# The first chunk of an LSH-attention and MLP kernel in two parts, and some conversion work on GpSimd

## The chip, the cores and the metric

The kernel runs on one core of a Trainium2 chip. The metric is the device time of one execution in microseconds (us). A core has five engines that run their own instruction streams and wait for one another by semaphores: TensorE (PE; its weight loads are listed apart as PEld), VectorE (DVE), ScalarE (ACT), GpSimd (POOL) and SyncE (SP), which here only starts transfers. Instructions of one engine run in the order in which they stand.

## The reference

```
q_bits = (q @ proj) > 0 ; k_bits = (k @ proj) > 0          # 6 bits each
mask   = bucket(q_bits)[:, None] == bucket(k_bits)[None, :]
scores = where(mask, q @ k.T / sqrt(64), -1e9)
attn   = softmax(scores) @ v
x      = attn of the 8 heads side by side                  # 3072 x 512
h      = x @ w_in ; g = where(h > 0, h, exp(min(h, 0)) - 1)
out    = g @ w_out
```

There are 4 batches, 8 heads, 768 rows, 64 values per head; `w_in` is 512 x 2048, `w_out` 2048 x 512. Inputs are float32, and the weights come as 64-bit floats of which the kernel makes 32-bit ones itself. The weight matrices, the MLP and the softmax are as in the reference; all matrix products run in 16-bit floats, each operand split into a hi part and a lo part (the rest), so that one product is three matmuls.

## The kernel before, in words

**Work items.** A *pair* is two heads of one batch; four pairs make a batch. A *chunk* is half of the rows of a batch (3 of its 6 tiles of 128 rows, `HC = 3`), for all four pairs; there are eight chunks. For each pair and chunk, `pair_part` does six tiles of attention (3 row tiles for each of two heads), two at a time (a *duo*): PE makes the scores (tile `ss` or `os`, lines 776 to 789), DVE copies them out of PSUM with their maximum (`top`, line 796), ACT takes the exponential (819), ACT makes the hi part of the normalised row (tile `hl`, line 844 through helper line 217), DVE the lo part (847 through helper line 220), and a transposing DMA on SP turns it into tile `PT`. When the six tiles have landed, PE multiplies with V (`av`, 867 to 879), and ACT and DVE make the hi and lo parts of `x` (888, 891).

**The experts (the MLP).** `moe_part` needs `x` of all four pairs of its chunk. For each of 16 slices `f` of the 2048 hidden columns PE makes `h` (12 matmuls, line 940), five elementwise steps follow (`e1` ACT 956, `e2` POOL 960, `e3` DVE 963, `e4` ACT, `e5` DVE through the helper lines 217 and 220), and PE adds to the three output tiles `o` (9 matmuls, line 988).

**The weights.** 32 blocks of 128 x 512 are loaded in `w_part` by SP into three or four buffers, decoded (ACT 695, DVE 699 and 703), bounded (PE `acc`, 714), and, when all 16 of one matrix have been bounded and its scale is known (`w0s`, `w1s`), split: hi on ACT, lo on DVE (745 to 752).

**Early work.** The first chunk's Q and K are turned by PE instead of DMA, and their hash bits are made by `bits_early`: PE multiplies with the projection into tile `zh` (line 481), DVE compares with zero (line 485). The projection itself is prepared by `prep_proj` (255 to 280), which starts with its own two small transfers, on ACT's queue.

**What sets the order.** Every step is a `job` with an engine, an estimated time, a key and what it waits for; `run_plan` (122 to 187) plays the jobs through with the constants of lines 31 to 48 (hops between engines, leads of the early loads, keys) and writes each engine's instructions in the order it finds. A change of a constant can so move any instruction.

## Time and profile before

| | us |
|---|---|
| median of 3 runs (lowest, highest) | 902.96 (902.17, 907.09) |
| the profiled execution | 905.69 |
| its span, first to last instruction | 903.9 |

| engine | busy us | share | instructions |
|---|---|---|---|
| PE | 821.7 | 91% | 5161 |
| DVE | 704.3 | 78% | 1482 |
| ACT | 699.1 | 77% | 1360 |
| POOL | 125.8 | 14% | 179 |

The page cuts the span into 40 slices of 22.6 us and prints a digit for each engine and slice: its busy share in tenths. A row of a table by stage gives, for a stretch of the span, the busy time of each engine with its number of instructions in brackets, then the granted TensorE clock (PEclk, 1.00 is full), the busy share of the DMA engines and what they moved. A row of a group of instructions gives line, engine, operation, the tile written and the tiles read, the shapes and the count; then the busy time of the group and the mean of one instruction in ns; then the idle time of the engine just before these instructions and what ended it.

### The profile page before, as it was taken

What the parts mean: (1) busy time and instruction counts of PE and PEld (TensorE: products, weight loads), DVE (VectorE), ACT (ScalarE), POOL (GpSimd) and SP (SyncE); (2) the same over time, 40 slices, a digit from 0 to 9 for tenths busy, and PEclk for the clock granted to TensorE, in tenths of its full rate; (3) what the DMA queues carried; (4) which work ended last, traced back from release to release, by engine and by line L of the source; (5) the groups of instructions that cost most, each with busy time, mean ns of one, the idle gap of its engine ahead of it and who ended that gap; (6) DMA issues with size and microseconds to landing.
All of it is one profiled execution on the core that took longest, in us unless ns stands there. A gap on an engine that the chain in (4) does not pass through costs nothing.

```text
span 903.9 us, 14772 instructions
## 1 busy us (share of the span) xinstructions
PE 821.7 (91%) x5161; PEld 431.0 (48%) x5161; DVE 704.3 (78%) x1482; ACT 699.1 (77%) x1360; POOL 125.8 (14%) x179
## 2 busy tenths in 40 slices
PE   2767565999999999999999999999999999999996
PEld 1323222454455555555554555545554555555553
DVE  4999999899696877898896977896986877773322
ACT  5978798999787878988976979897877878783332
POOL 1000000110012111211121112111211111111211
PEclk9777656999999999999999999999999999999999
DMA  8398898788878887797897898887876777652000
GB/s 278 123 258 221 217 232 196 133 166 152 143 142 161 149 175 170 158 172 129 147 189 128 175 177 147 179 144 150 144 162 135 134 115 149 114 106 39 36 1 35
DMA packets 391339, 135.11 MB, mean 149 GB/s; under 512 B 368001, under 2 KB 385633, under 8 KB 391265
## 3 DMA queue, kind: packets, MB, share of 16 engines
q1 hardware_dynamic: 389184, 127.88, 70.4%
q0 software_dynamic: 1920, 6.29, 1.9%
q8 instruction: 40, 0.66, 0.3%
q14 instruction: 35, 0.28, 0.1%
q10 hardware_dynamic: 160, 0.00, 0.0%
HBM read 35.65 MB, written 6.29 MB: 46 GB/s over the span
## 4 chain that ended last, share of the span: by engine, by line
PE 67%; DVE 18%; ACT 5%; DMA 5%; issue 4%; POOL 0%; SPq 0%; POOLq 0%; DVEq 0%; ACTq 0%
PE h L940 23%; PE o L988 23%; PE ss L782 10%; PE av L873 8%; DVE pt L796 4%; DVE hl L220 4%; DMA PT<-hl 2%; PE z L501 2%; DVE W L220 1%; DVE W L703 1%; ACT pt L819 1%; DVE K L485 1%; DVE W L699 1%; DMA pf<-in_proj_dram 1%; ACT hl L217 1%
## 5 line engine op out<-in xcount | busy, mean ns | idle before, releaser
L940 PE MATMUL h<-x,W 128*128 128x384 f16 x1536 | 283.4, 327 | 0.3 <-DVE U L963 0.3
L988 PE MATMUL o<-W,U 128*128 128x512 f16 x1152 | 281.0, 379 | 0.0
L796 DVE TENSOR_SCALAR_CACHE_REDUCE pt<-ss 128x768 f32<-128x768 f32 x180 | 170.9, 949 | 62.7 <-PE ss L782 55.6
L960 POOL TENSOR_SCALAR U<-U,ch 128x384 f32<-128x384 f32 x128 | 109.1, 852 | 740.2 <-ACT U L956 673.0
L940 PEld LDWEIGHTS <-W 128*128 128x128 f16 x1536 | 148.6, 98 | 115.9 <-issue 8.3
L220 DVE SCALAR_TENSOR_TENSOR hl<-pt,duo,hl 128x768 f16<-128x768 f32 x192 | 194.0, 1016 | 10.0 <-ACT hl L217 9.3
L819 ACT ACTIVATE pt<-pt,duo,sg 128x768 f32<-128x768 f32 x192 | 195.3, 1018 | 1.7
L217 ACT ACTIVATE hl<-pt,duo 128x768 f16<-128x768 f32 x192 | 176.3, 924 | 12.7 <-DVE duo L832 12.6
L782 PE MATMUL ss<-K,O 128*128 128x384 f16 x720 | 153.8, 337 | 17.0 <-DVE pt L796 16.7
L988 PEld LDWEIGHTS <-U 128*128 128x128 f16 x1152 | 110.9, 97 | 119.0 <-issue 5.6
L956 ACT ACTIVATE U<-h,ch 128x384 f32<-128x384 f32 x128 | 73.2, 572 | 59.1 <-PE h L940 58.4
L782 PEld LDWEIGHTS <-O 128*128 128x128 f16 (+1 forms) x768 | 73.6, 101 | 91.6 <-issue 37.6
L873 PE MATMUL av<-PT,vhl 128*64 128x384 f16 x1152 | 109.2, 346 | 3.6 <-DMA PT<-hl 3.6
L217 ACT ACTIVATE U<-U,ch 128x384 f16<-128x384 f32 x128 | 77.6, 606 | 41.7 <-DVE U L963 41.1
L963 DVE SCALAR_TENSOR_TENSOR U<-h,U 128x384 f32<-128x384 f32 x128 | 70.4, 550 | 42.2 <-POOL U L960 42.2
L220 DVE SCALAR_TENSOR_TENSOR U<-U,ch 128x384 f16<-128x384 f32 x128 | 78.7, 615 | 26.8 <-ACT U L217 26.3
L873 PEld LDWEIGHTS <-vhl 128*64 128x64 f16 x1152 | 66.9, 116 | 45.0 <-issue 12.4
L812 ACT ACTIVATE duo<-duo,sg 128x2 f32<-128x2 f32 x96 | 27.7, 289 | 34.3 <-DVE pt L796 34.2
L819 ACT ACTIVATION_READ_ACCUMULATOR pt<-pt,duo,sg 128x1 f32 x192 | 36.2, 188 | 0.0
L714 PE MATMUL acc<-W 128*128 128x128 bf16 x128 | 16.0, 270 | 20.2 <-DVE W L703 20.2
L510 DVE TENSOR_SCALAR zb<-z,pjt 64x384 f16<-64x384 f32 (+1 forms) x40 | 24.1, 602 | 1.8 <-PE z L501 1.8
L501 PE MATMUL z<-O,pjz 128*32 128x384 f16 (+1 forms) x168 | 22.0, 337 | 3.4 <-DVE x L891 3.2
(121 smaller groups left out, 557.0 us busy)
## 6 DMA issues: line engine op xcount, KB each, us to landing
U<-in_moe_w_in_dram SPq DMA_DIRECT2D x12, 512.0 KB
vf<-in_v_dram SPq DMA_DIRECT2D x16, 384.0 KB
U<-in_moe_w_out_dram SPq DMA_DIRECT2D x12, 512.0 KB
out_dram<-W POOLq DMA_DIRECT2D x24, 256.0 KB, 2.5
qst<-in_q_dram SPq DMA_DIRECT2D x30, 192.0 KB
kst<-in_k_dram SPq DMA_DIRECT2D x14, 384.0 KB
PT<-hl SPq DMA_TRANSPOSE x192
W<-in_moe_w_in_dram SPq DMA_DIRECT2D x4, 512.0 KB
```

What stands on the lines that cost most here:

```text
L217: nc.scalar.activation(o, x, AF.Copy, scale=s)
L220: nc.vector.scalar_tensor_tensor(o, x, s, hi, ALU.mult, ALU.subtract)
L501: nc.tensor.matmul(t[u * QD : (u + 1) * QD], pj["z"][:rows, zi, :], flat(st[src])[:rows, u * w : (u + 1) * w], start=n == 0, stop=n == len ...
L782: nc.tensor.matmul(t[:, x, :HALF], st[o][:rows, at, :], kst[kk][:rows, j * NC + x * HC : j * NC + (x + 1) * HC, :].rearrange("p a b -> p ( ...
L796: nc.vector.tensor_scalar(pt.rearrange("p (n e) -> p n e", n=2), box["s", at % 2][:, :, :HALF], CLAMP, None, ALU.max, ALU.max, accum_out=b ...
L819: nc.scalar.activation(pt, pt, AF.Exp, bias=u[:, 2 + i : 3 + i], scale=st["sg"][:, 0:1], accum_out=u[:, 4 + i : 5 + i])
L873: nc.tensor.matmul(av[j * D : (j + 1) * D], vst["v"][p][:, j, c, vx, :], PTs[j][:, :, px, c, :], start=n_ == 0 and c == 0, stop=n_ == 2 an ...
L940: nc.tensor.matmul(box["h"], WH[:, g * KT + t, wx, fc * P : (fc + 1) * P], xs[ns[t]][:, xx, :], start=t == 0 and i == 0, stop=t == KT - 1 ...
L956: nc.scalar.activation(box["e"], box["h"], AF.Exp, scale=css[b][:, 0:1])
L960: nc.gpsimd.tensor_scalar(box["e"], box["e"], css[b][:, 2:3], css[b][:, 3:4], ALU.mult, ALU.add)
L963: nc.vector.scalar_tensor_tensor(box["e"], box["h"], 0.0, box["e"], ALU.max, ALU.min)
L988: nc.tensor.matmul(banks[t][:, :DO], box["g"][:, gx, t * P : (t + 1) * P], WH[:, NSI + 1 + f, wx, :], start=f == 0 and i == 0, stop=f == N ...
```

## The change

1. **The first chunk in two parts.** `parts_of(0)` gives a thin part of one row tile (128 rows) and a part of two; all other chunks stay whole. All four pairs do the attention of the thin part first, then the experts can start on it, while the attention of the other two tiles goes on. For the thin part the experts take four slices `f` at a time (a PSUM bank of 4 x 128 columns), for the other part two (2 x 256), so the elementwise steps there work on 512 columns instead of 384. PE's matmuls for `h` and `av` of this chunk are split into ones of 128 and of 256 columns; the second matmul (`o`) has 128 rows and 512 columns as before.
2. **Work moved to GpSimd.** The hi parts of all weight blocks, of the first chunk's four K and four Q tiles, and of V of the last three batches are made by POOL (`scaled`) instead of ACT. The 20 hash comparisons of `bits_early` (DVE before) become a copy out of PSUM by ACT and a comparison by POOL.
3. **The projection.** Its two transfers are issued at the very start, and `prep_proj` becomes a job behind the first pair's scales.
4. **Buffers and constants.** Pairs 1 and 2 of the first chunk are scaled together (`FIRST`), `hl` gets buffers of its own, the fourth pair's O tiles borrow the place of two `x` tiles, and all constants of the planner are new.

```
-EAGER = 0.05
-AHEAD = 6.0
-HOP = {"PE": 0.25, "ACT": 0.30, "DVE": 0.37, "POOL": 0.30, "SP": 0.20}
-DMA_HOP = 1.50
+EAGER = 0.00
+AHEAD = 7.4
+HOP = {"PE": 0.27, "ACT": 0.30, "DVE": 0.23, "POOL": 0.37, "SP": 0.46}
+DMA_HOP = 1.06
...
-S_LAG = 5
+S_LAG = 9
+GP = {'w': 'POOL', 'v0': 'ACT', 'v': 'POOL', 'k0': 'POOL', 'k': 'ACT', 'q0': 'POOL', 'q': 'ACT', 'z0': 'POOL', 'kd': 'DVE', 'qd': 'DVE', 'kd0': 'DVE', 'qd0': 'DVE'}
+FIRST = ((0,), (1, 2), (3,))
...
+    def scaled(unit, o, x, s):
+        if unit == "ACT":
+            a_scaled(o, x, s)
+        else:
+            nc.gpsimd.tensor_scalar(o, x, s, 1.0, ALU.mult, ALU.mult)
...
     pj = {}
+    pf = const.tile([P, NB], F32, name="pf")
+    for j in range(2):
+        nc.scalar.dma_start(pf[j * D : (j + 1) * D, :], proj)
 
     def prep_proj():
-        pf = const.tile([P, NB], F32, name="pf")
-        for j in range(2):
-            nc.scalar.dma_start(pf[j * D : (j + 1) * D, :], proj)
...
-    proj_job = job("DVE", 2.6, prep_proj, -45)
-    proj_job.ready = 5.0
+    proj_job = []
...
+        def take_out():
+            bank["z"] = part("z")[:, :w]
+            nc.scalar.activation(bank["z"][used], bank["t"][used], AF.Copy)
+
+        def cmp_pool():
+            compare(nc.gpsimd, bank["z"])
+
         m = job("PE", 0.22 * len(ways), mm, key, after=after, take=("h",))
-        return job("DVE", 0.12 + w * 0.00108, cmp, key, after=(m,), give=("h",))
+        if GP["z0"] == "DVE":
+            return job("DVE", 0.12 + w * 0.00108, cmp, key, after=(m,), give=("h",))
+        c = job("ACT", 0.1 + w * 0.00085, take_out, key, after=(m,), take=("z",), give=("h",))
+        c = job("POOL", 0.1 + w * 0.0018, cmp_pool, key, after=(c,), give=("z",))
+        stage_jobs["z"].append(c)
+        return c
...
-            h = job("ACT", 0.61, hi, key, after=(scales[o], chain[o]))
-            chain[o] = w_ready[i] = job("DVE", 0.66, lo, key, after=(h,))
+            h = job(GP["w"], hi_us(GP["w"], SL), hi, key, after=(scales[o], w_ready.get(i - 2)))
+            w_ready[i] = job("DVE", 0.66, lo, key, after=(h,))
...
+    def parts_of(ci):
+        return ((0, 1, 4), (1, 2, 2)) if ci == 0 else ((0, HC, 1),)
...
+        if split:
+            duos = [(t, t + HC) for t in range(t0, t0 + nt)]
+        else:
+            duos = [(2 * d, 2 * d + 1) for d in range(PD)]
...
+            steps = [(0, (t,)) for t in range(KT)] if per == 1 else [(x, t) for x in range(per) for t in ((0, 1), (2, 3))]
...
+        for part_ in parts_of(ci):
+            moe_part(ci, order[n0][2], order[n0][4], [n0 + i for i in range(NP)], part_, base)
+            base += NF
```

Three places show what the planner made of it. The first is DVE around its first `e3` (the row that writes `U` from `h`), where the experts begin before; here the lo parts of `w_out` (rows `W<-W,w1s`) still have a long way to go. First as it was:

```order
L220 SCALAR_TENSOR_TENSOR W<-W,w1s 128x512
L510 TENSOR_SCALAR zb<-z,pjt 64x384
L796 TENSOR_SCALAR pt,duo<-ss 128x768
L220 SCALAR_TENSOR_TENSOR W<-W,w1s 128x512
L832 RECIPROCAL duo<-duo 128x2
L796 TENSOR_SCALAR pt,duo<-ss 128x768
L963 SCALAR_TENSOR_TENSOR U<-h,U 128x384
L220 SCALAR_TENSOR_TENSOR hl<-pt,duo,hl 128x768
```

In the change this is DVE around the last of the 16 lo parts of `w_out`; behind it stands the first `e3` of the second part.

```order
L239 SCALAR_TENSOR_TENSOR hl<-pt,duo,hl 128x768
L857 TENSOR_SCALAR pt,duo<-ss 128x768
L239 SCALAR_TENSOR_TENSOR W<-W,w1s 128x512 x2
L550 TENSOR_SCALAR zb<-z,pjt 64x384
L894 RECIPROCAL duo<-duo 128x2
L857 TENSOR_SCALAR pt,duo<-ss 128x768
L239 SCALAR_TENSOR_TENSOR W<-W,w1s 128x512
L239 SCALAR_TENSOR_TENSOR hl<-pt,duo,hl 128x768
L1045 SCALAR_TENSOR_TENSOR U<-h,U 128x512
```

What moved: seven lo parts of `w_out` stand ahead of the first `e3` before; in the change all 16 stand ahead of the `e3` that is shown, and the four `e3` and four `e5` of the thin part stand among them.

The second place is where the first chunk's hi parts are made. Before, they are ACT's instructions of line 217 (`natk`, `nat1q` and, for pairs 1 and 2, pieces of the big tile `W`):

```order
L217 ACTIVATE natk<-kst,qs 128x12x64
L217 ACTIVATE nat1q<-qst,qs 128x6x64
L217 ACTIVATE W<-W,qs 128x12x64
L217 ACTIVATE W<-W,qs 128x6x64
```

In the change they are POOL's, and POOL's comparisons (line 510, from a piece of `W` into the K2 and O2 tiles) stand among them:

```order
L227 TENSOR_SCALAR natk<-kst,qs 128x12x64
L227 TENSOR_SCALAR nat1q<-qst,qs 128x6x64
L227 TENSOR_SCALAR W<-W,qs 128x12x64 x2
L227 TENSOR_SCALAR W<-W,qs 128x6x64
L510 TENSOR_SCALAR K_208<-W,pjt 12x512 x2
L227 TENSOR_SCALAR W<-W,qs 128x6x64
L510 TENSOR_SCALAR K_208<-W,pjt 12x512
L510 TENSOR_SCALAR O_243<-W,pjt 12x512
L510 TENSOR_SCALAR O_243<-W,pjt 12x256
```

What moved: POOL's first work before is an `e2` of the experts; in the change 64 POOL instructions (8 hi parts of K and Q, 20 comparisons, 32 hi parts of weights, 4 `e2`) stand ahead of the second part's first `e2`.

The third place is the head of DVE's stream. Before, the projection (`pjx`, the row's maximum of `pf`) is first:

```order
L247 TENSOR_REDUCE pjx<-pf 128x1
L230 TENSOR_SCALAR pjm<-sum 128x1
L240 TENSOR_SCALAR pje<-pjm 128x1
L242 RECIPROCAL pjs<-pje 128x1
L243 TENSOR_SCALAR pjs<-pjs 128x1
```

In the change the scales of the first pair (`qm`, `ex`, `qs`, `sg`) come ahead of it:

```order
L394 TENSOR_SCALAR qm<-sum 128x1
L395 TENSOR_SCALAR qm<-qx 128x1
L396 TENSOR_SCALAR ex<-qm 128x2
L399 TENSOR_SCALAR ex<-ex 128x2
L401 RECIPROCAL qs<-ex 128x2
L402 TENSOR_SCALAR qs<-qs 128x2
L412 SCALAR_TENSOR_TENSOR sg<-ex 128x1 x2
L266 TENSOR_REDUCE pjx<-pf 128x1
```

What moved: seven rows of scales now stand ahead of the row that waits for the projection's transfer, and the hi parts on POOL wait for these scales alone.

More of the change, by code (lines that the diff above doesn't have):

```diff
@@ L313, in lsh_attention_moe @@
     guards.append((free[0], end, "v"))
+    end = free[0]
+    area["z"] = [flat(spare(1, 512)) for _ in range(2)]
+    guards.append((free[0], end, "z"))
     def nothing():
         pass
-    proj_job = job("DVE", 2.6, prep_proj, -45)
-    proj_job.ready = 5.0
+    proj_job = []
     ks, qs = {}, {}
@@ L415, in k_split @@
             ky = keys[2] + (1.0 * i if not early else 0.0)
-            j1 = job("ACT", 0.83, hi, ky, after=(made,), take=st["nat"])
+            eng = GP["k0" if early else "k"]
+            j1 = job(eng, hi_us(eng, S), hi, ky, after=(made,), take=st["nat"])
             j2 = job("DVE", 0.93, lo, ky, after=(j1,), give=() if own else ("kst",))
@@ L760, in pair_part @@
         kst, st = ks[b, p], qs[n]
-        last_scores = None
+        split = nt < HC
+        end = t0 + nt == HC
         landed = []
-        PTs = [None, None]
-        first_of_pair = True
-        for d in range(PD):
+        PTs = {}
+        queue.setdefault("scores", ())
+        queue.setdefault("tops", ())
+        queue.setdefault("turns", ())
+        if split:
+            duos = [(t, t + HC) for t in range(t0, t0 + nt)]
+        else:
+            duos = [(2 * d, 2 * d + 1) for d in range(PD)]
@@ L766, in pair_part, with scores @@
+        for d, duo in enumerate(duos):
             box = {"pt": [], "hl": []}
             tops, exs = [], []
-            at0 = 2 * d
-            last_duo = d == PD - 1
-            for i in range(2):
-                at = at0 + i
+            last_duo = end and d == len(duos) - 1
+            kd = key0 + d
+            for i, at in enumerate(duo):
                 j = at // HC
-                which = "s1" if ci == 0 and at % 2 else "s0"
-                def scores(at=at, j=j, which=which, box=box):
+                which = "s1" if ci == 0 and i else "s0"
+                def scores(i=i, at=at, j=j, which=which, box=box):
@@ L802, in pair_part @@
                 if last_duo and i == 1:
-                    give = ("O",) + (("K",) if c0 else ())
-                s = job("PE", 0.66, scores, D0 + d + OFF["S"], after=kst["ready"] + st["ready"], behind=(last_scores,),
+                    give = st["O"] + (("K",) if c0 else ())
+                s = job("PE", 0.66, scores, kd + OFF["S"], after=kst["ready"] + st["ready"], behind=queue["scores"],
                         take=(which,), give=give)
-                last_scores = s
-                tops.append(job("DVE", 0.88, top, D0 + d + OFF["M"], after=(s,), behind=tops,
+                queue["scores"] = (s,)
+                tops.append(job("DVE", 0.88, top, kd + OFF["M"], after=(s,), behind=tops or queue["tops"],
                                 take=("pt",) + (("duo",) if i == 0 else ()), give=(which,), mark=True))
@@ L925, in batch_scales, with moe_part @@
         vs[b]["cs"] = (j1, j2)
-    def moe_part(ci, b, c0, ns):
-        w = HC * P
-        for f in range(NF):
-            g, fc = f // FG, f % FG
-            seq = ci * NF + f
+    def moe_part(ci, b, c0, ns, part_, base):
+        t0, nt, per = part_
+        w = nt * P
+        wide = per * w
+        first_part, end = t0 == 0, t0 + nt == HC
+        cols = slice(t0 * P, (t0 + nt) * P)
+        unit = "w5" if per > 1 else "e"
+        for f0 in range(0, NF, per):
+            seq = base + f0
@@ L970, in e5 @@
                 v_rest(box["g"][:, 1, :], box["e"], css[b][:, 1:2], box["g"][:, 0, :])
-            ring = w_ready["decoded"] if seq < 4 else []
-            j1 = job("ACT", 0.47, e1, -100 + 1e-3 * seq, after=[prev, cs[0]] + ring, behind=(moe_last.get("e1"),), take=("e",))
+            ring = list(ring_free)
+            one = per == 1
+            j1 = job("ACT", k - 0.01, e1, -100 + 1e-3 * seq, after=[prev, cs[0]] + ring, behind=(moe_last.get("e1"),), take=(unit,))
             moe_last["e1"] = j1
-            j2 = job("POOL", 0.82, e2, -100 + 1e-3 * seq, after=(j1,))
@@ L976, in moe_part @@
-            j3 = job("DVE", 0.47, e3, -100 + 1e-3 * seq, after=(j2,), give=("h",))
-            j4 = job("ACT", 0.51, e4, -100 + 1e-3 * seq, after=(j3,), behind=(moe_last.get("e4"),), take=("g",))
+            j2 = job("POOL", 0.1 + 0.72 * wide / HALF, e2, -100 + 1e-3 * seq, after=(j1,))
+            j3 = job("DVE", k - 0.01, e3, -100 + 1e-3 * seq, after=(j2,), give=("h",))
+            j4 = job("ACT", k + 0.03, e4, -100 + 1e-3 * seq, after=(j3,), behind=(moe_last.get("e4"),), take=("g",) if one else ())
@@ L1024, in moe_part @@
             moe_last["S"] = prev
+            if not one and f0 + 3 * per >= NF and end:
+                ring_free.append(prev)
     order = []
@@ L1032, in lsh_attention_moe @@
                 order.append((len(order), len(order) // NP, b, p, c0))
[L1033 removed]
+    groups = [list(g) for g in FIRST] + [[n, n + 1] for n in range(NP, len(order), 2)]
     for ns in groups:
```

321 lines of the change are left out of this document (185 added, 136 removed).

## The prediction

> **What bounds the kernel now.** I read the 40 slices first, then a table by stage.
>
> ```profile
> span 903.9 us, 14772 instructions
> PE   2767565999999999999999999999999999999996
> DVE  4999999899696877898896977896986877773322
> PEclk9777656999999999999999999999999999999999
> 10.00:160.00 150.00, 94.76 (x558) 46.53 (x557) 142.30 (x335) 123.08 (x230) 0.00 (x0) 0.72 0.83 214
> 160.00:180.00 20.00, 19.19 (x131) 10.23 (x130) 17.25 (x33) 19.97 (x45) 3.23 (x4) 1.00 0.76 133
> 180.00:896.00 716.00, 707.73 (x4476) 374.10 (x4474) 544.62 (x1116) 549.45 (x1075) 117.71 (x145) 1.00 0.71 135
> 896.00:903.90 7.90, 0.00 (x0) 0.00 (x0) 0.12 (x1) 1.37 (x2) 1.67 (x3) 0.79 0.26 100
> ```
>
> There are two stages. From 160 to 896 PE works 727 of 736 us at full clock: only less PE work, or PE work done earlier, shortens it. Before 160 PE works 95 of 150 us at a clock of 0.72, and DVE works 142 of 150: DVE is the bound. What DVE waits for in this stage:
>
> ```profile
> DVE pjx L247 <- DMA pf<-in_proj_dram: 11.0, 1, 11.0
> DVE W L220 <- ACT W L217: 2.6, 4, 1.1
> ```
>
> So DVE starts at 11 us, because of the projection's transfer, and then hardly waits. The switch between the stages is the experts' first matmul, and the end of PE's work is the last `o`:
>
> ```profile
> 161.41 2.60 PE L940 MATMUL h<-x,W 128*128 128x384 f16 x15
> 889.99 5.99 PE L988 MATMUL o<-W,U 128*128 128x512 f16 x27
> ```
>
> From 161.4 to 896.0 are 734.6 us, and 7.9 follow in which the last rows leave. The experts must wait for attention of a whole chunk, 12 duos, on a DVE that also decodes and splits all weights. The change asks for a third of that attention first.
>
> **One point to count from.** In the change I take the first `o` matmul of slice 15 of the thin part. It needs the last lo part of `w_out`, so it follows the second order shown on DVE; behind it PE has work enough, as before behind 161.4. By the order of PE, what stands ahead of it is what stood ahead of the first `h` before (all turns, bounds, the whole chunk's `av`, all hash bits), and beyond that: 192 `h` of 128 columns, 24 of 256, 45 `o` and 8 score matmuls. Their prices in the saturated stage:
>
> ```profile
> 882.37 1.94 PE o L988 x9
> 884.31 1.96 PE h L940 x12
> ```
>
> 0.216 us for an `o`, 0.163 for an `h` of 384 columns. The 192 thin ones are 64 wide ones of work (10.4 us), the 24 are 16 (2.6), the 45 `o` are 9.7, the 8 scores, also 384 columns, 1.3: PE is 24.0 us ahead. If that `o` starts at T, PE ends at T + 734.6 - 24.0, and the span is T + 718.5. **Break-even is T = 185.4.** The `h` of 256 columns that remain cost 0.109, two thirds of 0.163, hence no more in all. Thin ones are dearer than a third, since a weight load takes as long as in the next row, but they lie ahead of T.
>
> ```profile
> L940 PEld LDWEIGHTS <-W 128*128 128x128 f16 x1536 | 148.6, 98 | 115.9 <-issue 8.3
> ```
>
> **T by DVE.** Before, DVE reached its first `e3` at 167.0. These are its groups up to there that I use:
>
> ```profile
> L220 DVE SCALAR_TENSOR_TENSOR hl<-pt,duo,hl 128x768 f16<-128x768 f32 x28 | 28.2, 1012 | 0.2
> L703 DVE SCALAR_TENSOR_TENSOR W<-U,W 128x512 int32<-128x512 int32 x24 | 16.2, 684 | 0.0
> L703 DVE SCALAR_TENSOR_TENSOR W<-W 128x512 int32<-128x512 int32 x8 | 5.5, 686 | 0.1
> L220 DVE SCALAR_TENSOR_TENSOR W<-W,w0s 128x512 f16<-128x512 f32 x16 | 11.9, 744 | 0.0
> L220 DVE SCALAR_TENSOR_TENSOR W<-W,w1s 128x512 f16<-128x512 f32 x7 | 5.2, 747 | 2.0 <-ACT W L217 2.0
> L485 DVE TENSOR_SCALAR K<-zh,pjt 12x512 f16<-12x512 f32 x12 | 8.8, 747 | 0.3
> L485 DVE TENSOR_SCALAR O<-zh,pjt 12x512 f16<-12x512 f32 x4 | 3.0, 746 | 0.1
> L485 DVE TENSOR_SCALAR O<-zh,pjt 12x256 f16<-12x256 f32 x4 | 1.9, 479 | 0.1
> L374 DVE TENSOR_SCALAR ex<-qm 128x2 int32<-128x2 int32 x6 | 1.0, 169 | 0.2
> 167.00 0.56 DVE L963 SCALAR_TENSOR_TENSOR U<-h,U 128x384 f32<-128x384 f32 x1 [0.53 <-POOL U L960]
> L220 DVE SCALAR_TENSOR_TENSOR U<-U,ch x128: 597/614/869, 170.1 to 892.9; 128x384 f16<-128x384 f32 x128
> ```
>
> In the change the same 32 `top`, 28 `hl`, 32 decodes and 16 lo parts of `w_in` stand ahead of the last lo part of `w_out`. Gone are the 20 comparisons (8.8 + 3.0 + 1.9 = 13.7) and one group of 8 small scale instructions (8 x 0.16 = 1.3). New are 9 more lo parts of `w_out` (9 x 0.747 = 6.7), 4 `e3` and 4 `e5` on 512 columns ((0.56 + 0.614) x 512/384 x 4 = 6.3) and 0.3 for `x` in two pieces. Sum: -1.7. That last lo part then takes 0.7, and a hop to PE about 0.3 (an estimate: 0.28 is the `e3` to `h` wait of this trace): T = 167.0 - 1.7 + 1.0 = 166.3, if nothing else changes.
>
> *Start.* The scales of the first pair wait for the square of Q:
>
> ```profile
> 5.64 0.19 ACT L251 ACTIVATION_READ_ACCUMULATOR nat1q<-qst 128x1 f32 x1
> 14.67 0.93 ACT L217 ACTIVATE natk<-kst,qs 128x768 f16<-128x768 f32 x1 [5.68 <-DVE qs L380]
> ```
>
> DVE can begin at 5.9 instead of 11.0 (-5.1); the projection's transfers are issued at once, with five microseconds to land. But the hi parts now come from one POOL queue. By the POOL rows below, 768 elements take 1.32 there (2 x 0.66) against 0.93, and ahead of the sixth hi part stand five others and two comparisons; DVE will wait for the later ones. I give 1.6 back: -3.5, T = 162.8. The bounds are -5.1 and 0.
>
> *POOL and DVE.* Up to T POOL gets 64 instructions where it had none:
>
> ```profile
> L960 POOL TENSOR_SCALAR U<-U,ch x128: 652/662/1882, 166.3 to 890.9; 128x384 f32<-128x384 f32 x128
> L960 POOL TENSOR_SCALAR U<-U,ch 128x384 f32<-128x384 f32 x22 | 18.6, 845 | 269.1 <-ACT U L956 246.9 <-ACT duo L828 22.3
> 195.43 0.73 POOL L960 TENSOR_SCALAR U<-U,ch 128x384 f32<-128x384 f32 x1 [4.17 <-ACT duo L828]
> 195.64 1.33 DVE L220 SCALAR_TENSOR_TENSOR natk<-kst,qs,natk 128x768 f16<-128x768 f32 x1
> 200.22 1.18 POOL L960 TENSOR_SCALAR U<-U,ch 128x384 f32<-128x384 f32 x1 [4.06 <-ACT U L956]
> 200.96 0.98 DVE L220 SCALAR_TENSOR_TENSOR W<-W,w1s 128x512 f16<-128x512 f32 x1
> ```
>
> The first is the shortest, middle and longest of all, the second the group from 161 to 300. Alone it takes 0.66; behind a DVE instruction that reads two SBUF tensors it waits (1.18), and such a DVE instruction that starts while POOL runs is held: 1.33 where 768 elements take 1.01, 0.98 where 512 take 0.745. By 0.66 for 384 elements, the 64 are 55 us of POOL alone (28.2 weights, 15.8 comparisons, 7.9 K and Q, 3.5 `e2`). From 161 to 300, 22 POOL instructions (14.5 us alone) held DVE four times, 0.9 us in all: 6%, with two-input work in some 45% of DVE's time. In the head it is some 55% (the rows above and the other lo parts), DVE never idles, and a longer POOL instruction holds longer. From below: 6% of 55, 3 us. From above: every overlap held in full, 55 x 0.55 = 30. Nearest are the 22: 6% times 1.2 for the share and about 1.5 for the length give 6, and I take 8.
>
> The Trainium skill (Advanced Engine Details and Errata, GPSIMD Details) says the same of the cause: the Pool engine shares a read and a write interface with DVE and conflicts with DVE instructions that have two SBUF inputs. It names no price; if sharing meant strict exclusion, the upper bound would be the sum, and that is a rival below.
>
> *New waits.* The fourth pair's five comparisons stand behind five hi parts on POOL, and its `top` behind them; ACT gets 20 copies (some 10 us, by the 0.75 and 0.48 that DVE took) but loses 16 + 16 weight hi parts and eight K and Q ones. The last decode stands at 66% of this DVE work instead of 79%, so loads are wanted some 20 us earlier, with the DMA engines at 0.83 in this stage and 12 instead of 18 turns ahead of them. I add 2.5 for all of it, bounds 0 and 12.
>
> T = 162.8 + 8 + 2.5 = 173.3; **span 891.8**, 12.1 us less. The profiled execution took 905.7 with 903.9 of span; the median is 902.96, so I forecast **891**.
>
> At nothing: V's hi parts of later batches on POOL (24 x 0.66 = 16 us), the new constants, the copy of `hl` buffers. From 180 on PE is busy 708 of 716 and POOL 118; uncovered they could cost or save about the 8 us that PE idles there.
>
> **Rivals.**
>
> *POOL holds DVE in full.* 30 instead of 8 us: T = 162.8 + 30 + 2.5 = 195.3, span 913.8, **913 us, slower**. It decides from 20.1 us on (break-even), which is 36% of POOL's 55 us. For it: both held rows above, and a head with DVE back to back. Against: 6% measured. [...]
>
> *POOL costs DVE nothing and no new wait comes*: T = 162.8 + 1, span 882.3, **881**. For it: 18 of the 22 POOL instructions held nobody.
>
> *PE becomes the bound between its first `h` and T.* The fourth thin `x` stands at 51% of this DVE work, so the first `h` comes at about 11 + 0.51 x 156 - 3.5 + 7 = 94. From there to T are about 60 us of PE work at full clock (192 thin `h` at 0.10, 76 scores, 45 `o`, four `av` of 256 columns, 32 bounds, 24 `h`). Covered by the 79 us that DVE takes; but at the clock of 0.72 of this stage it is 83 us, and with waits for DVE in between T = 183: span 901.5, **901, no change**. For it: PEclk falls to 0.5 to 0.7 in the head. Against: from 160 to 180 a busy PE got 1.00.
>
> *The change doesn't do what it says*: the thin part is ready early but its `o` waits for `w_out`, since `w1s` comes late. That is in the sum (T is this wait).
>
> **Chances.** Forecast 0.52 (own range 884 to 898), POOL free 0.18, PE bound 0.18, POOL holds DVE 0.12. About 0.5% (4.5 us) is what can be told from no change: faster 0.70, same 0.18, slower 0.12. The range takes in the free POOL and most of the no-change case, and leaves out the slow one: 878 to 904.
>
> **What would show it.** Right: first `e3` on 512 columns near 120, the last `W<-W,w1s` near 172, DVE busy over 90% from 10 to 165, PE saturated from 173 with 9 us idle behind, `hl` and `W` lo parts longer than 1.01 and 0.745 by about 8 us in all, DVE starting near 6. Wrong: T beyond 185; DVE idling for POOL by more than 5 us; PE losing more than 12 us after T; or the projection's transfer still landing near 11.

## The result: 1.3% slower, and the profile after

The changed kernel took 916.57 us in the median of four runs (915.11 to 917.39), against 904.47 for the kernel before, also in four runs; the ratio is 1.0132 (95% interval 1.0109 to 1.0154). Forecast were 891 us, with a range of 878 to 904. The profiled execution took 915.1 with 913.3 of span, 9.4 more than before.

The table by stage, in the same columns as for the kernel before (length, then busy time and count of PE, PEld, DVE, ACT and POOL, the granted clock, the DMA share, GB/s):

```profile
10.00:60.00 50.00, 36.76 (x186) 17.67 (x187) 36.71 (x80) 39.92 (x72) 37.28 (x21) 0.78 0.67 220
60.00:180.00 120.00, 84.73 (x768) 54.58 (x767) 111.43 (x226) 87.82 (x173) 52.37 (x41) 0.79 0.77 181
220.00:300.00 80.00, 68.51 (x459) 36.90 (x456) 70.10 (x147) 63.69 (x125) 16.57 (x18) 0.94 0.83 165
5.21:184.19 178.98, 125.81 (x977) 74.50 (x977) 156.40 (x339) 133.26 (x257) 93.34 (x65) 0.80 0.76 197
184.24:906.08 721.84, 703.25 (x4519) 377.66 (x4517) 547.30 (x1112) 539.14 (x1051) 139.57 (x165) 0.99 0.71 136
```

and the rows of the kernel before that answer to the first and to the last three:

```profile
10.00:60.00 50.00, 30.91 (x187) 16.09 (x187) 46.30 (x120) 40.22 (x75) 0.00 (x0) 0.84 0.70 206
220.00:300.00 80.00, 75.50 (x470) 39.37 (x468) 63.84 (x142) 62.41 (x125) 12.44 (x15) 0.96 0.81 149
11.04:167.00 155.96, 101.27 (x597) 50.13 (x597) 147.68 (x346) 130.05 (x246) 0.66 (x1) 0.73 0.84 212
161.41:895.98 734.57, 725.61 (x4597) 383.74 (x4594) 560.44 (x1146) 568.01 (x1116) 120.94 (x149) 1.00 0.71 135
```

Two things are off. DVE, which idled 3.7 us from 10 to 60 before (50.00 - 46.30), idles 13.3 us there now. And PE, behind the point T that the forecast counts from, idles 18.6 us (721.84 - 703.25) where it idled 9.0 before (734.57 - 725.61); 11.5 of them lie between 220 and 300, where it was 4.5. Over the whole execution PE is busy 7.6 us longer (829.3 for 821.7), and it idles 76.8 us up to the end of its work where it idled 74.3 before: the early experts fill idle time in the head, and as much comes back behind it. PE's timeline shows T, and then the place of the second loss:

```profile
184.24 0.81 PE L1076 MATMUL o<-W,U 128*128 128x512 f16 x3
184.89 4.09 PE L1017 MATMUL h<-x,W 128*128 128x256 f16 x36
...
233.79 0.82 PE L1017 MATMUL h<-x,W 128*128 128x256 f16 x6
...
239.73 0.81 PE L843 MATMUL ss<-K,O 128*128 128x384 f16 x4 [1.16 <-DVE pt L857]
...
253.07 1.46 PE L843 MATMUL ss<-K,O 128*128 128x384 f16 x4 [3.89 <-DVE pt L857]
...
264.74 0.65 PE L1017 MATMUL h<-x,W 128*128 128x384 f16 x3
```

T is 184.2, not 173.3. And the first chunk's `h` end at 234.6 while the second chunk's first `h` (the first of 384 columns) starts at 264.7: for 30 us PE has only scores, `av` and remaining `o` to do, and waits for DVE between the scores.

**Where the first loss comes from.** The costliest groups of POOL up to 200:

```profile
L510 POOL TENSOR_SCALAR K<-W,pjt 12x512 f16<-12x512 f32 x12 | 27.7, 2314 | 0.8 <-ACT W L520 0.3
L227 POOL TENSOR_SCALAR W<-W,w1s 128x512 f16<-128x512 f32 x16 | 19.4, 1219 | 23.2 <-DVE W L239 16.5 <-DVE we L785 2.8 <-PE ss L843 2.4
```

and, from the list of waits between 10 and 183 (us in total, times, longest), what waited for the comparisons and what waited for that:

```profile
ACT W L520 <- POOL K L510: 11.5, 11, 2.3
DVE W L749 <- ACT W L745: 8.1, 3, 3.6
ACT W L745 <- POOL x L510: 4.2, 1, 4.2
```

A comparison of 512 columns that writes a K2 tile takes 2.31 us on POOL in the mean; the forecast priced it by `e2` at 0.88. ACT copies the hash products out for them (line 520) into two buffers, and a third copy stands until POOL has freed one: 11 of the 20 copies waited so. Behind such a copy, on ACT, stand decodes of weights, and DVE waits for those. From the timelines of POOL, ACT and DVE, one such knot:

```profile
42.82 11.29 POOL L510 TENSOR_SCALAR K<-W,pjt 12x512 f16<-12x512 f32 x5
54.09 6.84 POOL L510 TENSOR_SCALAR O<-W,pjt 12x512 f16<-12x512 f32 x4
...
47.66 0.59 ACT L520 ACTIVATE W<-zh 12x512 f32<-12x512 f32 x1 [0.95 <-POOL K L510]
49.79 0.59 ACT L520 ACTIVATE W<-zh 12x512 f32<-12x512 f32 x1 [0.39 <-POOL K L510]
50.40 0.66 ACT L745 ACTIVATE W<-W 128x512 f32<-128x512 f32 x1
...
51.09 0.43 DVE L749 TENSOR_SCALAR W<-W 128x512 int32<-128x512 int32 x1 [3.20 <-ACT W L745]
```

### The profile page after: what moved, and what is told of

The parts are those of the page before. It is cut to its first block, busy times and chain, and to the rows that moved or that the text cites. A ratio compares the mean times of both kernels' runs of the same rounds, so it can differ in the third digit from the quotient of the medians.

```text
span 913.3 us, 15739 instructions
## 1 busy us (share of the span) xinstructions
PE 829.3 (91%) x5496; PEld 452.4 (50%) x5496; DVE 703.8 (77%) x1450; ACT 676.3 (74%) x1312; POOL 237.6 (26%) x259
## 4 chain that ended last, share of the span: by engine, by line
PE 56%; DVE 14%; issue 9%; ACT 7%; POOL 5%; DMA 5%; SPq 2%; POOLq 0%; DVEq 0%; ACTq 0%
PE h L1017 20%; PE o L1076 19%; PE ss L843 9%; PE av L939 7%; DVE hl L239 4%; DVE pt L857 4%; POOL K L510 3%; ACT pt L881 2%; PE z L541 1%; DMA qst<-in_q_dram 1%; ACT hl L221 1%; DMA U<-in_moe_w_in_dram 1%; DVE W L239 1%; DMA PT<-hl 1%; POOL U L1042 1%
## 5 line engine op out<-in xcount | busy, mean ns | idle before, releaser
L1017 PE MATMUL h<-x,W 128*128 128x384 f16 (+2 forms) x1728 | 286.7, 311 | 1.2 <-DVE U L1045 1.2
L1042 POOL TENSOR_SCALAR U<-U,ch 128x384 f32<-128x384 f32 (+1 forms) x124 | 112.5, 907 | 518.5 <-ACT U L1038 408.2
L221 ACT ACTIVATE hl<-pt,duo 128x768 f16<-128x768 f32 x192 | 175.7, 925 | 26.5 <-DVE duo L894 20.2
L221 ACT ACTIVATE U<-U,ch 128x384 f16<-128x384 f32 (+1 forms) x124 | 76.6, 618 | 53.8 <-DVE U L1045 40.6
L843 PEld LDWEIGHTS <-O 128*128 128x128 f16 x744 | 71.2, 101 | 88.7 <-issue 38.6
L1045 DVE SCALAR_TENSOR_TENSOR U<-h,U 128x384 f32<-128x384 f32 (+1 forms) x124 | 69.8, 563 | 50.0 <-POOL U L1042 50.0
L239 DVE SCALAR_TENSOR_TENSOR U<-U,ch 128x384 f16<-128x384 f32 (+1 forms) x124 | 77.9, 628 | 38.3 <-ACT U L221 38.2
L939 PE MATMUL av<-PT,vhl 128*64 128x384 f16 (+2 forms) x1296 | 104.5, 317 | 1.2 <-DMA PT<-hl 1.1
L1038 ACT ACTIVATE U<-h,ch 128x384 f32<-128x384 f32 (+1 forms) x124 | 71.9, 581 | 45.2 <-PE h L1017 44.5
L939 PEld LDWEIGHTS <-vhl 128*64 128x64 f16 x1296 | 71.4, 115 | 33.6 <-issue 10.6
L227 POOL TENSOR_SCALAR W<-W,w0s 128x512 f16<-128x512 f32 x16 | 18.4, 1155 | 42.4 <-DVE W L239 20.1
L510 POOL TENSOR_SCALAR K<-W,pjt 12x512 f16<-12x512 f32 x12 | 27.7, 2314 | 0.8 <-ACT W L520 0.3
```

The costliest lines, as they stand in the source:

```text
L221: nc.scalar.activation(o, x, AF.Copy, scale=s)
L239: nc.vector.scalar_tensor_tensor(o, x, s, hi, ALU.mult, ALU.subtract)
L510: eng.tensor_scalar(flat(st[x2])[used, a : a + w], src[used], pj["thr"][used, which : which + 1], (MBIT, -MBIT)[which], ALU.is_gt, ALU.mult,)
L843: nc.tensor.matmul(t[:, x, :HALF], st[o][:rows, at, :], kst[kk][:rows, j * NC + x * HC : j * NC + (x + 1) * HC, :].rearrange("p a b -> p ( ...
L939: nc.tensor.matmul(av[j * D : (j + 1) * D], vst["v"][p][:, j, c, vx, :], pt[:, :, px, c, :], start=n_ == 0 and c == 0, stop=n_ == 2 and c ...
L1017: nc.tensor.matmul(box["h"][:, x * w : (x + 1) * w], WH[:, g * KT + t, wx, fc * P : (fc + 1) * P], xs[ns[t]][:, xx, cols], start=x == 0 an ...
```

## The experiments

Two theories to begin with. A: the comparisons are dear on POOL and hold ACT and, through it, DVE. B: POOL holds DVE at what they share, or loads come late. For the second loss, C: the thin part itself leaves PE without work behind T. "Fixed order" below means that the planner is untouched, so that every instruction but the edited ones stands where it stood; the other kernels were ordered anew.

**1. Another operation in the comparisons, fixed order.**

```diff
-                (MBIT, -MBIT)[which], ALU.is_gt, ALU.mult,
+                (MBIT, -MBIT)[which], ALU.mult if eng is nc.gpsimd else ALU.is_gt, ALU.mult,
```

> The change with its order untouched; only the operation inside the 20 early comparisons on POOL is another (multiply in place of is-greater-than), so the hash bits of the first chunk, and with them its mask, are not the reference's. A (the comparisons cost 2.26 us each on POOL where 0.88 was forecast; ACT, whose copies have two buffers, waits for them, and DVE waits for ACT, 14 us more than forecast): if the new operation takes 0.9 us or less, T (184.2 in the change) comes at about 170, and the span falls from 913.3 by 14 to about 899, or to 890 if the 11 us that PE idles more behind T are a consequence of the same delay. B (the delay is from POOL holding DVE at their shared port, or from loads that come late): DVE's idle time before T stays above 15 us, T above 180, span 908 or more. If a comparison takes 2 us or more with the other operation too, the operation isn't what costs, and the run decides nothing else.

908.15 us, ratio 1.0048 (1.0027 to 1.0070); span 905.6. The same instruction with a multiplication takes half the time (shortest, median and longest in ns, first and last start; the line of the change, then that of the experiment):

```profile
L510 POOL TENSOR_SCALAR K<-W,pjt x12: 1987/2262/2895, 17.7 to 76.4; 12x512 f16<-12x512 f32 x12
```

```profile
L510 POOL TENSOR_SCALAR K<-W,pjt x12: 688/1046/1844, 17.7 to 67.5; 12x512 f16<-12x512 f32 x12
```

T in PE's timeline, and two rows of the table by stage (DVE's from its first instruction to T, and the hole):

```profile
174.33 0.81 PE L1076 MATMUL o<-W,U 128*128 128x512 f16 x3
```

```profile
5.21:174.28 169.07, 123.47 (x977) 74.64 (x977) 158.65 (x339) 133.52 (x257) 75.03 (x65) 0.80 0.80 207
220.00:300.00 80.00, 68.70 (x441) 36.73 (x441) 68.67 (x144) 64.59 (x127) 15.49 (x16) 0.94 0.84 158
```

At its shortest the comparison takes 1.99 us and the multiplication 0.69. T falls by 9.9 to 174.3, a microsecond from the forecast's 173.3, and DVE's idle time up to T from 22.6 to 10.4 us. A holds for this part in place and direction, though not in size: it gave T at about 170 and a span of 899, and the span is 905.6. B falls for this part (it gave T above 180 and over 15 us of idle DVE). The second loss is untouched: 11.3 us of idle PE from 220 to 300, and the second chunk's first `h` 31 us behind the first chunk's last. So A doesn't explain it.

**2. The comparisons on DVE again.**

```diff
-GP = {'w': 'POOL', ..., 'z0': 'POOL', ...
+GP = {'w': 'POOL', ..., 'z0': 'DVE', ...
```

> The change with the 20 early comparisons on DVE out of PSUM again, as before the change (the planner orders anew). A: DVE gets 13.7 us of work back and loses 14 us of waits and about 4 us of holds: T about 180, span 898 if PE idles behind T as little as in the kernel before (8 us), 909 if as much as in the change (19 us). B (port): T falls by 4 at most but for the 13.7 it gains: T about 194, span 920.

908.40 us, ratio 1.0058 (1.0037 to 1.0079), span 906.2. That is on the side of A with the idle time of the change behind T, which gave a span of 909, though T is at 174.4 and not at 180: DVE waits 0.7 us for hash products and next to nothing for decodes, and PE idles 14.8 us from 220 to 300.

**3. One part instead of two, and 4. the thin part without POOL's new work.**

```diff
 # whole
-        return ((0, 1, 4), (1, 2, 2)) if ci == 0 else ((0, HC, 1),)
+        return ((0, HC, 1),)
 # all_back
-GP = {'w': 'POOL', ..., 'v': 'POOL', 'k0': 'POOL', ..., 'q0': 'POOL', ..., 'z0': 'POOL', ...
+GP = {'w': 'ACT', ..., 'v': 'ACT', 'k0': 'ACT', ..., 'q0': 'ACT', ..., 'z0': 'DVE', ...
```

> The change with the first chunk in one part (parts_of gives one part for all chunks); POOL's work and all constants stay. A: the waits of the comparisons stay (+14), port holds stay (+8), the 13.7 us of comparisons are off DVE and the start is 5.8 earlier: first e3 at about 167.0 - 13.7 - 1.3 - 5.8 + 8 + 14 = 168, span about 905, and PE idles some 8 us behind its first h, as before. C (the thin part costs by itself, in PE's waits behind T): span under 900. D (the thin part does bring its 24 us of PE work ahead, and the move to POOL is what costs): span 913 to 930.

> The change with all of POOL's new work back on ACT and DVE (weights, K, Q, V, comparisons); the thin part, the early projection and the constants stay. A: T = 184.2 - 14 (waits) - 8 (holds) + 13.7 (comparisons) = about 176, span 894.5 if PE idles 8 us behind T, 905 if the 19 us of the change are the thin part's own. D (POOL's new work costs nothing net, the thin part is what costs): T 184 or later, span 913 or more.

whole: 917.33 us, ratio 1.0150 (1.0120 to 1.0179). all_back: 907.64 us, ratio 1.0057 (1.0031 to 1.0084). whole is in the range of D; A missed there, with the first `e3` at 182.5 and not at 168. In all_back D missed, and so did the place of T: it came at 163.8, where A gave 176, and the span was 908.1 all the same, near the 905 that A gave for a thin part that keeps its idle time. (Its order is another, and leaves PE 716.8 us of work behind T, 13.6 more than in the change.) With POOL's work, one part is as slow as two; so the thin part gains nothing net, though it does bring PE work ahead (the first `h` comes at 107.4 in the change and at 176.7 in whole). PE's idle time tells why: from 100 to 180 it is 36.2 us in whole and 18.2 in the change, from 220 to 300 it is 4.2 in whole and 11.5 in the change. Moving POOL's work back gives 7 to 11 us, new orders included.

**5. The early projection alone, in the kernel before.**

```diff
+    pf = const.tile([P, NB], F32, name="pf")
+    for j in range(2):
+        nc.scalar.dma_start(pf[j * D : (j + 1) * D, :], proj)
...
-    proj_job = job("DVE", 2.6, prep_proj, -45)
-    proj_job.ready = 5.0
+    proj_job = []
...
+        if n0 == 0:
+            proj_job.append(job("DVE", 2.5, prep_proj, keys[1], behind=(made,)))
```

> The kernel before with only the projection changed: its transfers are issued first, and its preparation stands behind the first pair's scales (the planner orders anew). By the forecast's term for the start, DVE begins 5 us earlier and T, here the first h at 161.4, comes 5 us earlier: about 156, span 899. Rival: what DVE gains at the start it waits for later, or the new order costs it: first h at 160 or later, span 903 or more.

895.74 us, ratio 0.9904 (0.9874 to 0.9933): faster than both kernels. DVE begins at 5.29 instead of 11.04,

```profile
5.29 0.16 DVE L372 TENSOR_SCALAR qm<-sum 128x1 f32<-128x1 f32 x1 [5.29 <-PE sum L371]
```

and the first `h` comes at 158.8 instead of 161.4, not at the expected 156, while the span of 895.4 is below the expected 899. The 2.6 us are part of the 8.5 us of the span; most of the rest is behind the first `h` (728.7 us to the end of the last `o` instead of 734.6), where the new order leaves PE less work and less idle time. How much of that is owed to the projection, and how much to an order that happened to be better, this run can't say.

**6. to 8. The planner's constants.** whole_back is the change with one part and without POOL's new work; whole_old is the same with the constants of the kernel before; thin_old0 has those constants and the thin part.

```diff
 # whole_back: GP as in all_back, parts_of as in whole
 # whole_old: whole_back, and
-EAGER = 0.00
-AHEAD = 7.4
+EAGER = 0.05
+AHEAD = 6.0
...
-S_LAG = 9
+S_LAG = 5
 # thin_old0: whole_old with parts_of as in the change
```

> The change without its thin part and without POOL's new work: what is left are the early projection, the other constants of the planner and the pools. If the constants cost nothing: as before_pf, span about 899. If the constants (tuned for another plan) cost: 903 or more, and that share is the change's too.

> whole_back (one part, no new work on POOL) with the twelve lines of the planner's constants of the kernel before; what is left of the change are the early projection, the pairs 1 and 2 of the first chunk prepared together, and the pools. If the constants cost the 11 us between before_pf (895.7) and whole_back (906.6): about 896. If the joint preparation and the pools cost them: 905 or more.

> all_back (the thin part and the early projection, POOL's new work back on ACT and DVE) with the twelve lines of the planner's constants of the kernel before. If the new constants are what made all_back as slow as 907.6: 897 or less, and the thin part brings something beside the projection (895.7 in before_pf) only if it is under 893. If the thin part costs by itself whatever the constants: 905 or more.

whole_back: 906.56 us, ratio 1.0026 (1.0009 to 1.0043). whole_old: 894.93 us, ratio 0.9896 (0.9873 to 0.9918). thin_old0: 908.07 us, ratio 1.0046 (1.0030 to 1.0063). All three came out as expected for constants that cost and for a thin part that costs. The order that the new constants give costs 12 us without the thin part and nothing with it (907.6 and 908.1). The thin part costs 13 us under the old constants and 1 to 3 under the new. The stretch from 220 to 300 of thin_old0 and of whole_old shows the same hole again:

```profile
220.00:300.00 80.00, 67.56 (x426) 34.32 (x424) 64.63 (x139) 62.77 (x122) 8.66 (x10) 0.94 0.80 145
```

```profile
220.00:300.00 80.00, 79.11 (x526) 42.22 (x525) 63.26 (x136) 60.58 (x122) 15.08 (x17) 1.00 0.74 143
```

12.4 us of idle PE with the thin part, 0.9 without.

**9. What POOL alone costs DVE, fixed order.** In the kernel before, POOL gets work that nothing waits for.

```diff
...
             def recip(box=box):
                 nc.vector.reciprocal(u[:, 6:8], u[:, 6:8])
+                if n < NP:
+                    for _ in range(12):
+                        nc.gpsimd.tensor_scalar(idle_o, idle_i.to_broadcast([P, 12, 16]), u[:, 6:7], 1.0, ALU.mult, ALU.mult)
```

> The kernel before, its order untouched, with 144 more POOL instructions that nothing waits for: behind each of the 12 reciprocals of the first chunk's attention 12 that multiply 192 columns (a small tile read again and again, into a scratch tile). They make POOL busy for an estimated 50 us in the head, about as long as the 64 of the change by the forecast's reckoning, and add no wait. By the forecast's price (8 us held for 55 us of POOL) the first h comes 5 to 9 us later than 161.4 and the time rises by as much, to about 911. If POOL held DVE in full: up to 30 us, 930. If POOL holds nobody: no change, and DVE's two-input instructions keep their 1.01 and 0.745 us.

911.70 us, ratio 1.0076 (1.0050 to 1.0101): 6.9 us, and the first `h` at 168.7. The added instructions were longer than estimated, 0.75 instead of 0.35 us in the mean, so that POOL was busy 107 us in the head, not 50. The groups of POOL and of DVE up to 170, with the shortest, median and longest of the added ones in ns, and one of DVE's groups as it was before:

```profile
L838 POOL TENSOR_SCALAR idle_o<-idle_i,duo 128x192 f16<-128x192 f32 x144 | 107.4, 746 | 52.0 <-DVE duo L835 38.7
L838 POOL TENSOR_SCALAR idle_o<-idle_i,duo x144: 424/603/2024, 42.2 to 163.1; 128x192 f16<-128x192 f32 x144
```

```profile
L223 DVE SCALAR_TENSOR_TENSOR hl<-pt,duo,hl 128x768 f16<-128x768 f32 x28 | 30.0, 1076 | 0.2
L223 DVE SCALAR_TENSOR_TENSOR W<-W,w0s 128x512 f16<-128x512 f32 x16 | 12.8, 802 | 0.0
L702 DVE TENSOR_SCALAR W<-W 128x512 int32<-128x512 int32 x32 | 14.0, 452 | 0.1
```

```profile
L699 DVE TENSOR_SCALAR W<-W 128x512 int32<-128x512 int32 x32 | 12.9, 417 | 0.1
```

DVE's instructions stretch (1.076 for 1.012, 0.802 for 0.744, 0.452 for 0.417), and 7 us is what it comes to: 6 to 7% of POOL's busy time. That is as late as was expected, but for twice the POOL time, so the forecast's price of a us of POOL was about twice too high. So the rival by which POOL holds DVE in full falls, and B with it, as far as POOL is meant. What the 107 us also show is that the conflict falls on POOL for the most part: the shortest of the 144 takes 0.42 us; the 52 with next to no two-input instruction of DVE (SCALAR_TENSOR_TENSOR) beside them have a median of 0.425, and the 75 with one beside them for at least half of their time one of 1.00. At 0.42 each they would be 61 us, so some 46 us are POOL's own delay (an estimate from these rows), against DVE's 7.

**10. to 13. What sets the second chunk's start.** If DVE, or DVE and the transposing transfers, pace the second chunk's attention while PE has run out of experts, taking that work off them must bring its first `h` forward. relief and relief2 are at fixed order on top of experiment 1; relief_before is the control in the kernel before.

```diff
 # relief, relief_before: second chunk only
-                    v_rest(box["hl"][i][:, 1, :], box["pt"][i], box["duo"][:, 6 + i : 7 + i], box["hl"][i][:, 0, :])
+                    k = P if ci == 1 else S
+                    if ci == 1:
+                        nc.gpsimd.memset(box["hl"][i][:, 1, k:], 0.0)
+                    v_rest(box["hl"][i][:, 1, :k], box["pt"][i][:, :k], box["duo"][:, 6 + i : 7 + i], box["hl"][i][:, 0, :k])
 # relief2: that without the memset, and
+                    if ci == 1:
+                        nc.gpsimd.memset(flat(PTs[buf][:, slot, 1]), 0.0)
+                        nc.sync.dma_start_transpose(PTs[buf][:, slot, 0], box["hl"][i][:, 0, :])
+                        return
```

> fast_cmp (multiply in place of the 20 comparisons) and one thing more: for the second chunk the lo part of the normalised rows is made for 128 of its 768 columns, the rest is set to zero by POOL; so the second chunk's rows lose their lo parts, and the order of all else stays. It takes about 24 x 0.75 = 18 us off DVE between T and the second chunk's first h. S (PE, 24 us ahead, runs out of experts before DVE has finished the second chunk's attention, and DVE sets the pace there): the second chunk's first h of 384 columns comes over 8 us earlier than in fast_cmp, PE's idle time from 220 to 300 falls from 11.3 to 5 or less, span about 898. O (PE's waits come from the planner's fixed order or from transfers, not from DVE's load): idle time stays at 9 or more, span 904 or more.

> The kernel before with the same cut in the second chunk's lo parts (128 of 768 columns, the rest set to zero by POOL). S: here PE never runs out of experts, so 18 us less of DVE's work in the same stretch bring at most the 3 us that PE waits for DVE there: span 900 to 904. If it falls by over 5 us, DVE's load costs the kernel before as well, and S does not explain the difference.

> fast_cmp with more taken off the second chunk's attention than in relief: its lo parts are made for 128 of 768 columns, and only its hi parts are turned by transfer, half of each transfer's bytes (POOL sets the lo half of the target to zero); so the second chunk loses its lo parts. That is 18 us off DVE and some 20 us off the queue of transposing transfers, between T and the second chunk's first h of 384 columns, which came at 255.9 in fast_cmp and at 254.7 in relief. S2 (PE has run out of experts and attention as a whole sets the pace; in relief the transfers took DVE's place): that h comes before 248, PE's idle time from 220 to 300 falls from 11.3 to 5 or less, span under 900. O (the order in which PE's work is fixed makes the waits): 253 or later, idle 9 or more, span 902 or more.

relief: 905.35 us, ratio 1.0019 (1.0000 to 1.0037). relief_before: 904.80 us, ratio 1.0010 (0.9991 to 1.0030). relief2: 904.72 us, ratio 0.9989 (0.9972 to 1.0005). In relief and relief2 the second chunk's first `h` comes at 254.7 and 252.8, against 255.9, and PE idles 10.0 and 9.0 us from 220 to 300, against 11.3; that is the edge of what was expected for O, and far from S. Of the 18 us, 12 to 14 lay between T and that `h` (DVE's `hl` rows there take 9.9 and 11.2 us, where they took 23.7). In relief2, DVE was busy 30.9 of 40 us from 180 and 66.2 of 80 us from 220, the DMA engines 57% and 72%, and PE still waited (the table by stage, then PE's timeline):

```profile
180.00:220.00 40.00, 40.00 (x312) 24.41 (x310) 30.85 (x77) 34.13 (x67) 13.51 (x19) 1.00 0.57 111
220.00:300.00 80.00, 71.02 (x477) 39.09 (x474) 66.22 (x148) 65.78 (x129) 20.33 (x25) 0.96 0.72 137
```

```profile
237.23 0.17 PE L393 MATMUL sum<-kx,ones 128*128 128x2 bf16 x1
240.54 0.82 PE L843 MATMUL ss<-K,O 128*128 128x384 f16 x4 [3.15 <-DVE pt L857]
242.81 1.44 PE L843 MATMUL ss<-K,O 128*128 128x384 f16 x4 [1.44 <-DVE pt L857]
```

So neither DVE's load nor the transfers' alone sets it at this order: up to 220 PE itself is full (40.00 of 40), about half of it with the first chunk's experts, and its two longest waits between there and the second chunk's first `h` are scores that wait for the copying out of an earlier one; the first of these stands on DVE behind the scales that PE's `sum` releases. Together they have a share, though: by the ratios relief is 0.3% faster than experiment 1 (hardly clear of the noise) and relief2 0.6% (5 us), while the control shows no change.

**14. and 15. The same cut, with the planner told of it** (thin_relief on thin_old0, whole_relief on whole_old):

```diff
-                l = job("DVE", 0.93, lo, kd + OFF["L"], ...
+                l = job("DVE", 0.25 if ci == 1 else 0.93, lo, kd + OFF["L"], ...
-                                  ..., give=("hl",), move=2.2))
+                                  ..., give=("hl",), move=1.1 if ci == 1 else 2.2))
```

> thin_old0 (thin part, the old constants, no new work on POOL) with relief2's cut in the second chunk (lo parts made for 128 of 768 columns, only hi parts turned by transfer, POOL sets the lo halves to zero, so the second chunk loses its lo parts), and the planner told of it (DVE 0.25 instead of 0.93, transfer 1.1 instead of 2.2), so that the order follows, which it could not in relief and relief2. In thin_old0 the experts of the first chunk ended at 229.7, the second chunk's first h came at 265.0, and PE idled 12.4 us from 220 to 300. S3 (the second chunk's attention sets when its experts can begin, and a fixed order had only hidden that): first h of the second chunk at 256 or earlier, idle 6 or less, span 897 or less. O3 (the thin slices' order makes PE's waits whatever attention costs): 262 or later, idle 10 or more, span 902 or more.

> whole_old (one part, the old constants) with the same cut and the planner told of it: the control. S3: PE never ran out of experts there (0.9 us idle from 220 to 300), so a faster second chunk can bring 3 us at most: span 891 to 896. If it falls below 888, the cut is worth something of itself and thin_relief must be read against it.

thin_relief: 904.21 us, ratio 0.9988 (0.9972 to 1.0004), 0.6% faster than thin_old0; its second chunk's first `h` came at 262.0 (265.0 in thin_old0), and PE idled 9.5 us from 220 to 300. whole_relief: 908.40 us, ratio 1.0033 (1.0015 to 1.0051), 12 to 13 us slower than whole_old although it has less to do, where a span of 891 to 896 was expected. A cheaper second chunk gives some 5 us and doesn't close the hole even where the order can follow: the numbers lie on the side of O3, but for the idle time, which is just under its 10 us. And the control, which missed, warns of something else: one new order may cost 13 us by itself. So differences of that size between kernels that were ordered anew, the 12 us of the constants and the 13 us of the thin part among them, belong to a pair of orders and not to one edit; in this last pair the thin part is even 0.5% faster. What does not hang on one order is the hole. PE's idle time from 220 to 300, from the same view for each kernel:

| pair | with the thin part | without |
|---|---|---|
| the change, whole | 11.5 | 4.2 |
| all_back, whole_back | 12.7 | 0.0 |
| thin_old0, whole_old | 12.4 | 0.9 |
| thin_relief, whole_relief | 9.5 | 1.5 |

The fixed window isn't what makes the difference: counted from T to the end of the last `o`, PE idles 17.1 to 20.2 us in the eight kernels with the thin part; counted from the first `h`, it idles 3.3 to 14.1 us in the eight without.

## Why the prediction was wrong, step by step

The span was forecast at 891.8 and is 913.3. Of these 21.5 us, 10.9 are a later T (184.2 for 173.3) and 10.6 a longer way from T to the end (729.1 for 718.5); each has a step of its own that failed.

**T, term by term.** By the two rows from DVE's first instruction to T (5.21 to 184.19, and 11.04 to 167.00):

| step of the forecast | forecast | measured |
|---|---|---|
| earlier start of DVE | -5.1 | -5.8 |
| DVE's own work (-1.7, and 0.7 for the last lo part) with POOL's holds (8) | +7.0 | +8.7 (156.40 - 147.68) |
| waits: for POOL's hi parts (1.6), new ones (2.5) | +4.1 | +14.3 (22.6 - 8.3) |
| hop to PE | +0.3 | +0.05 |
| T | 173.3 | 184.2 |

**The start** was right: DVE begins at 5.21. Experiment 5 has this edit alone and is faster than both kernels, though with a new order.

**POOL's holds** came out at the forecast's size, but by luck. In the change and in all_back the same instructions read:

```profile
L239 DVE SCALAR_TENSOR_TENSOR hl<-pt,duo,hl 128x768 f16<-128x768 f32 x28 | 29.3, 1059 | 1.7 <-ACT hl L221 1.6
L753 DVE SCALAR_TENSOR_TENSOR W<-U,W 128x512 int32<-128x512 int32 x24 | 17.8, 753 | 2.9 <-DMA U<-in_moe_w_out_dram 2.7
L239 DVE SCALAR_TENSOR_TENSOR W<-W,w0s 128x512 f16<-128x512 f32 x16 | 12.7, 809 | 1.1 <-POOL W L227 1.1
L749 DVE TENSOR_SCALAR W<-W 128x512 int32<-128x512 int32 x32 | 14.3, 456 | 8.1 <-ACT W L745 8.1
```

```profile
L239 DVE SCALAR_TENSOR_TENSOR hl<-pt,duo,hl 128x768 f16<-128x768 f32 x30 | 30.3, 1011 | 1.2 <-ACT hl L221 1.1
L753 DVE SCALAR_TENSOR_TENSOR W<-U,W 128x512 int32<-128x512 int32 x24 | 16.4, 686 | 0.2
L239 DVE SCALAR_TENSOR_TENSOR W<-W,w0s 128x512 f16<-128x512 f32 x16 | 11.8, 747 | 0.8 <-ACT W L221 0.8
L749 DVE TENSOR_SCALAR W<-W 128x512 int32<-128x512 int32 x32 | 12.9, 419 | 0.6 <-ACT W L745 0.5
```

1.3 + 1.6 + 1.0 + 1.2 us in these four, and by the same reckoning 0.9 in the lo parts of `w_out` and some 2 in those of V, Q and K: about 8, for 93 us of POOL. The forecast had 8 for 55 us of POOL, so its price was too high (15% of POOL's busy time, where the rows give 9% and experiment 9 gives 6 to 7%) and its busy time too low, and the two errors cancelled. The rival of full holds (913 us) came near the measured time for another reason; at 30 us of holds DVE would have been busy where it idled. The Trainium skill (Advanced Engine Details and Errata, GPSIMD Details) names two kinds of DVE instruction that conflict with POOL, those with two SBUF inputs and those in a 2-port performance mode; the last of the four has one input and stretched too, which agrees with the second kind, though no run here shows in which mode it was.

**The waits** were the first step that failed, and within it the price of a comparison: 0.66 us for 384 elements was carried over from `e2`, another operation, to a comparison, which takes 1.99 at its shortest where a multiplication in its place takes 0.69. The 20 cost POOL 42.3 us (27.7 + 6.0 + 4.1 + 3.4 + 1.1), not 15.8. With that, POOL was busy 37.3 of 50 us from 10 to 60, and ACT's copies waited 11.5 us for its two buffers. Experiment 1 gives the size: 9.9 us of T, and 8.4 of the time. A second term was put at nothing: what DVE's two-input instructions cost POOL. The hi parts of the weights took 1.16 to 1.22 us on POOL in the mean, where 0.88 was forecast and the shortest took 0.69; DVE waited little for them (1.1 us), so by DVE's waits this made POOL's busy time larger and T hardly later.

**"Behind it PE has work enough, as before behind 161.4"** was the second step that failed. With T where it was forecast (experiment 1: 174.3) the span was 905.6 and not 892.8 (T + 718.5): PE idled 18.9 us behind T instead of 9.0, and it worked 705.1 there (of 723.95) and not 725.6 - 24.0 = 701.6; of the 12.8 us, 9.9 and 3.5 are these, and 0.6 came back in the tail. The sum took the busy share of PE behind 161.4 as a stock of work that stays; but the 24 us that the thin part takes out of it are for the most part experts of the first chunk, and those are the only experts that can fill PE until the second chunk's `x` is there. That point came no earlier for the thin part: the second chunk's first `h` came at 264.7 in the change and at 252.8 to 268.5 in the other seven kernels with it, and at 258.7 in the kernel before and 255.0 to 272.5 in the other seven without. (At the fixed order of experiment 1 it moved with T, 8.8 us for 9.9, and the hole stayed.) In PE's timelines the longest stretch without an `h` between 200 and 330 is 6.5 to 14.1 us in the eight kernels without the thin part, and 27 to 44 in the eight with it. What was brought ahead of T was missing there, and 12.8 of the 24.0 us were given back. That DVE was busy 120 of 140 us from 160 to 300 before could have been read as a warning, and no more than that, since experiments 10 to 15 don't bear out DVE's load as the one cause: of PE's 134 us in the same stretch the change takes 24 away, which leaves 110, less than DVE's 120.

What exactly sets the second chunk's start is open. DVE's load and the transposing transfers are excluded as single causes by experiments 10 to 15, and taking both off gave some 5 us; the chain of waits changes between PE, DVE, ACT, POOL and transfers there at every few microseconds. That the missing experts make the hole is therefore an argument from the pairs of kernels, not the result of a run that put them back at a fixed order. No run took away the short waits between PE's scores and DVE themselves.

**The rival of PE at a low clock** did not come about as such: PE worked 125.8 of 179.0 us up to T, at a clock of 0.80, and in experiment 1, with the same PE work and a clock of 0.80, T came 10 us earlier. **That the change doesn't do what it says**: it does, the first `h` came at 107 and the first `o` at 149.5, but to no profit.

**What was to show it.** Right: DVE starting near 6 (5.2), T not beyond 185. Right in the sum alone: DVE's instructions stretched by about 8 us, but the `hl` and `W` lo parts, which were named, have only 3.3 of them. Wrong: DVE busy 86% from 10 to 165 instead of over 90 (73% from 10 to 60), the first `e3` on 512 columns at 136 instead of 120, the last `W<-W,w1s` at 183.5 instead of 172, PE losing 18.6 us behind T instead of 9.

## What to carry to other kernels

Work that is brought ahead of a bound is a gain only if the next point that must be waited for comes earlier too; before counting it, look which work fills the bounding engine up to that point, and whether another engine could deliver it sooner. Price a moved instruction by its operation, not by its size: the nearest row is one with the same operation on the same engine, and where none is there, the range must reach to a multiple. Where a planner orders everything anew after each edit, one edit's own price can only be read at a fixed order.
